# ACT instead of SP issues the eleven writes of the second group's first transform

## The chip, the cores and the metric

The kernel runs on one core of one Trainium2 chip. The metric is the time of one execution in microseconds (us). The engines are named as in the profile: PE (matrix multiplication, with PEld for its weight loads), DVE (elementwise), ACT (activation functions and copies), POOL (here index work and the transfers with indices) and SP (here only an issuer of transfers). Each engine works through its own instructions strictly in their order. A transfer (DMA) is issued by an engine and then runs on the core's 16 DMA engines; a trailing q (SPq, ACTq) marks such issues and waits in the rows.

## What is computed

The kernel first convolves each of 8 sequences of 2496 tokens with a filter in the frequency domain, and then sends every token through the one expert of 8 that a router picks for it:

```python
def _attn_ref(x, filt_r, filt_i):                  # x: 8 x 2496 x 256
    X = np.fft.rfft(x, axis=1)
    F = (filt_r + 1j * filt_i)[None, :, :]
    return np.fft.irfft(X * F, n=x.shape[1], axis=1)

def _moe_ref(x, expert_emb, tau, w1, w2):          # x: 19968 x 256
    ...
    logits = xn @ en.T / tau                       # normalized tokens and experts
    expert_idx = np.argmax(logits, axis=1)
    ...
    for e in range(E):                             # E = 8, F = 1024
        mask = expert_idx == e
        h = np.maximum(x[mask] @ w1[e], 0.0)
        out[mask] = gate_w[mask, None] * (h @ w2[e])
```

## The kernel before, in words

**Groups and transforms.** The 8 sequences are 8 groups (numbered 0 to 7), one sequence each. The Fourier transform over 2496 = 64 x 39 points is made of two small dense transforms in each direction, so that a group passes through three stages, which hand data to each other through scratch tensors in device memory:

- `conv_s1(g)`, the first transform, 11 steps: a tile of x is loaded (tiles `in`, L395), multiplied on PE (L435), copied out of PSUM by ACT into a tile `st` (L461, printed as `s`), and written to the scratch tensor SD (L463). This L463 is what the change touches.
- `conv_s2(g)`, 10 steps: a tile `a` is read back from SD (L475), multiplied (L435), filtered on DVE with a filter tile `f` (L482), transformed back (L551) and written to ZD (L555).
- `conv_sb(g)`: reads ZD, makes the token rows `y`, routes them, and POOL scatters the rows into a table XS ordered by expert (L787).

**Experts.** Tokens are then taken from XS in blocks ("slots"). A slot's rows are read transposed by SP (tile `xT`, for the first eight slots `xTf`, L867) with a small tile `meta` (`metaf`, L868) of row numbers and gate weights. PE multiplies them with the first weight matrix (`ph`, L955), ACT and DVE make the two halves of `h` (L961, L962), PE multiplies with the second matrix (`po`, L975), ACT scales (L982), and POOL scatters the result to the output (L983).

**The head.** While group 0 and the first transform of group 1 are worked off, no expert work is there yet; this stretch is `head()`. In it SP also loads the expert weights, 1 MB at a time (L257, tile W, 14 of them; the last expert's come as 8 pieces `wraw`, L264), and PE (L279, L289: `gram`), DVE (L284, L285, L293 to L300, L324) and ACT (L317) split each matrix into a high and a low 16-bit half. The expert work may use a matrix only after that. After the head, slots and the stages of the later groups alternate in `run_slots()`, group g+1's transforms beside group g's slots.

**What sets the order.** Each engine's order of instructions is decided when the kernel is built, by a scheduler that places instructions by estimated times; in the head the order on ACT, PE, DVE and SP follows the code. Each engine then waits on semaphores. Two rules matter here. The tiles rotate: `cin` has 4 buffers, so the load of tile t+3 in `conv_s1` waits until PE has used tile t-1; `st` has 3 buffers, shared with the tile `dg` of the weight preparation. And the transfers that SP and ACT issue share eight completion semaphores in turn, so that an issue also waits until the transfer that had its semaphore last has landed.

The four lines of `conv_s1` on which it turns:

```python
            st = cst.tile([P, 2, D], F32, tag="st", name=f"s{g}_{t}")
            nc.scalar.copy(st, pt)
            for h, k, m in whole(g, buf_at(g, SD[g]), t, freqs, 120):
                nc.sync.dma_start(m, st[:k, h])
```

Of the kernel before, what the change touches and what calls it, by code (L numbers as in the profile page):

```python
# [66 lines left out]
def full_blocks(tokens, size):  # L67

    return max(0, -((E * (size - 1) - tokens) // size))
# [3 lines left out]
def moe_spectral_kernel(  # L73
# [17 lines left out]
    nc = tc.nc  # L91
# [11 lines left out]
    for g, (n, size) in enumerate(GROUPS):  # L103
# [4 lines left out]
        k = full_blocks(least, size)  # L108
# [247 lines left out]
    def widths(g):  # L356

        return NAG * GROUPS[g][0] // 2, NK2 * GROUPS[g][0] // 2


    def whole(g, ap, t, rows, full):

        if GROUPS[g][0] == 2:
            k = rows(t)
            return [(slice(0, 2), k, ap(t, k, False))]
        if rows(2 * t) == rows(2 * t + 1):
            return [(slice(0, 2), full, ap(t, full, False))]
        return [(slice(j, j + 1), rows(2 * t + j), ap(2 * t + j, rows(2 * t + j), True)) for j in range(2)]

    def x_at(g):  # L370
        def at(t, k, half):
            if GROUPS[g][0] == 2:
                return x[first[g]:first[g] + 2, t * TOK:t * TOK + k].rearrange("b p c -> p b c")
            if half:
                return x[first[g], t * TOK:t * TOK + k].unsqueeze(1)
            return x[first[g], t * 2 * TOK:(t + 1) * 2 * TOK].rearrange("(j p) c -> p j c", j=2)
        return at

    def buf_at(g, buf):
        def at(t, k, half):  # L380
            if GROUPS[g][0] == 2:
                return buf[t * 120:t * 120 + k].rearrange("p (j c) -> p j c", j=2)
            if half:
                return buf[t * 120:t * 120 + k].unsqueeze(1)
            return buf[t * 240:(t + 1) * 240].rearrange("(j p) c -> p j c", j=2)
        return at
# [4 lines left out]
    def load(q, g, pool, tag, t, ap, rows, full):  # L391
        it = pool.tile([P, 2, D], F32, tag=tag, name=f"{tag}{g}_{t}")
        got = []
        for h, k, m in whole(g, ap, t, rows, full):
            q.dma_start(it[:k, h], m)  # L395
            got.append((h, it[:k, h].rearrange("p j c -> p (j c)")))
        return got
# [3 lines left out]
    def split(hi, lo, pieces):  # L401

        got = []
        for h, a in pieces:
            k, w = a.shape
            o = h.start * D
            xh, xl = hi[:k, o:o + w], lo[:k, o:o + w]
            nc.scalar.copy(xh, a)  # L408
            nc.vector.tensor_tensor(out=xl, in0=a, in1=xh.bitcast(F32), op=ALU.subtract)  # L409
            got.append((h, (xh, xl)))  # L410
        return got

    def pair(nm):
        return [cw.tile([P, 2 * D], F32R, tag="hl", bufs=XYB, name=f"{nm}_{i}") for i in range(2)]
# [6 lines left out]
    def parts_of(c, tag):  # L421

        k = c.shape[0]
        tmp = cw.tile([P, P], F32R, tag="hl", bufs=XYB, name=f"{tag}t")[:k]
        lo = const.tile([k, P], F32R, tag=f"{tag}l", name=f"{tag}l")
        nc.scalar.copy(tmp, c)
        nc.vector.tensor_tensor(out=lo, in0=c, in1=tmp.bitcast(F32), op=ALU.subtract)
        hi = const.tile([k, P], F32R, tag=tag, name=f"{tag}h")
        nc.scalar.copy(hi, tmp.bitcast(F32))
        return hi, lo  # L430

    def product(out_, c, a):

        if not isinstance(a, tuple):
            nc.tensor.matmul(out_, c[:a.shape[0]], a, start=True, stop=True)  # L435
            return
        (ch, cl), (xh, xl) = c, a
        k = xh.shape[0]
        for n, (w, b) in enumerate(((ch, xh), (cl, xh), (ch, xl))):
            nc.tensor.matmul(out_, w[:k], b, start=(n == 0), stop=(n == 2))  # L440

    def conv_s1(g):

        NTL, _ = widths(g)
        if g == G_S1:
            cons["c1"] = parts_of(cons["c1"], "c1")
        xin = {t: load(nc.gpsimd if g > 1 else nc.sync, g, cin, "in", t, x_at(g), tokens, TOK) for t in range(INB - 1)}
        if g == 1:
            yield 0
        for t in range(NTL):  # L450
            if t + INB - 1 < NTL:
                xin[t + INB - 1] = load(nc.gpsimd if g > 1 else nc.sync, g, cin, "in", t + INB - 1, x_at(g), tokens, TOK)
            if g >= G_S1:
                u = t
                xin[u] = split(*pair(f"xp{g}_{u}"), xin[u])
            pool, tag = (ps_h, "h") if g == 1 else (ps_c, "c")
            pt = pool.tile([P, 2, D], F32, tag=tag, name=f"s1_{g}_{t}")
            for h, xt in xin.pop(t):
                product(pt[:, h].rearrange("p j c -> p (j c)"), cons["c1"], xt)
            st = cst.tile([P, 2, D], F32, tag="st", name=f"s{g}_{t}")  # L460
            nc.scalar.copy(st, pt)  # L461
            for h, k, m in whole(g, buf_at(g, SD[g]), t, freqs, 120):
                nc.sync.dma_start(m, st[:k, h])  # L463
            yield W_S1

    def conv_s2(g):
# [533 lines left out]
    def later(g):  # L1000

        yield from conv_s2(g)
        if g + 1 < NG:
            s1 = conv_s1(g + 1)
            yield from both(conv_sb(g), s1, widths(g + 1)[0] / (2 * widths(g)[0] + 8))
            yield from s1
            yield -1
            yield from later(g + 1)
        else:
            yield from conv_sb(g)  # L1010
            yield -1
# [14 lines left out]
    def head():  # L1026
        yield from conv_s1(0)
        yield from conv_s2(0)
        back, ahead = conv_sb(0), conv_s1(1)
        for n, w in enumerate(back):  # L1030
            if n == XNEXT - 35:
                next(ahead)
            routed = state["routed"] * CHUNK * 2 >= NAG
            if routed and not queue:
                enqueue(0, "fixed")
            yield w
            if n >= SIDE:
                next(ahead, 0)
        yield from ahead
# [161 lines left out]
```

## Time and profile before

| | us |
|---|---|
| median of 3 runs | 1465.01 (1461.64 to 1469.56) |
| the profiled execution | 1456.85 |
| its span, first to last instruction | 1455.1 |
| PE busy | 1287.7 (88% of the span) |
| DVE busy | 958.9 (66%) |
| ACT busy | 760.4 (52%) |
| POOL busy | 512.7 (35%) |

The span starts at the first instruction of the program, and all places below are us from that start. The profiled execution is 0.56% shorter than the median; 1.75 us of it lie outside the span. Issuing a transfer does not count as busy time. A busy PE is one with a matmul in its pipeline, at either of its two clock levels (PEclk 1.00 is 2.4 GHz, 0.50 is 1.2 GHz). In a row of the timeline, a duration over several merged instructions (x5) runs from the start of the first to the end of the last, waits between them included; the brackets tell how long the engine had been idle before, and what ended that.

### The profile page before, as it was taken

The page shows a single profiled execution, that of the slowest core. Times are in us where ns is not written, and L with a number is a line of the kernel's source. Part 1 is how long each engine was busy: PE and PEld are TensorE (multiplying, and loading weights), DVE is VectorE, ACT ScalarE, POOL GpSimd, SP SyncE. Part 2 cuts the span into 40 slices and gives each one's busy share as a digit, 9 for nine tenths or more (in the row PEclk, how much of TensorE's full clock was granted, in tenths as well). Part 3 has the DMA queues.
Part 4 walks back from the last instruction along what each step waited for, and adds up shares of the span by engine and source line. Part 5 has one row for each costly group of instructions (what it writes and reads, how often), then busy time and mean ns, then how long its engine had stood idle before and what let it go on. Part 6 is the DMA issues. An engine that isn't in the chain of part 4 may idle for free. (4 is left out here: it accounts for less than half of the span.)

```text
span 1455.1 us, 36608 instructions
## 1 busy us (share of the span) xinstructions
PE 1287.7 (88%) x11006; PEld 999.8 (69%) x11006; DVE 958.9 (66%) x3126; ACT 760.4 (52%) x1756; POOL 512.7 (35%) x575
## 2 busy tenths in 40 slices
PE   6766799789877997999899988999899987999998
PEld 2243566556655775777688767877787776888997
DVE  2365796465757684978679776877686764444664
ACT  2264477345735683668456764676376622233333
POOL 0024022444344433542454245424532344112222
PEclk9877999889988997999999999999999989999999
DMA  7898879568747784779467966776575323211121
GB/s 234 285 343 295 214 223 212 149 189 235 179 122 210 211 180 118 208 187 201 120 178 208 190 145 167 220 194 157 156 195 163 93 73 73 60 45 52 42 45 41
DMA packets 275838, 240.64 MB, mean 165 GB/s; under 512 B 167946, under 2 KB 218001, under 8 KB 273857
## 3 DMA queue, kind: packets, MB, share of 16 engines
q1 hardware_dynamic: 249144, 180.33, 48.2%
q0 software_dynamic: 25360, 57.51, 12.7%
q8 instruction: 104, 1.70, 0.5%
q14 instruction: 85, 0.70, 0.2%
q10 hardware_dynamic: 1145, 0.40, 0.1%
HBM read 121.68 MB, written 85.90 MB: 143 GB/s over the span
## 5 line engine op out<-in xcount | busy, mean ns | idle before, releaser
L975 PE MATMUL po<-W,h 128*128 (+1 forms) x3864 | 517.0, 278 | 24.9 <-issue 20.4
L955 PE MATMUL ph<-xT,wp 128*128 128x256 f16 (+1 forms) x4224 | 494.5, 264 | 33.7 <-issue 23.1
L955 PEld LDWEIGHTS <-wp 128*128 128x128 f16 x4224 | 369.4, 100 | 122.9 <-issue 68.2
L975 PEld LDWEIGHTS <-h 128*128 128x128 f16 x3864 | 370.8, 99 | 106.7 <-issue 59.0
L961 ACT ACTIVATE h<-ph 128x512 f16<-128x512 f32 (+1 forms) x384 | 204.6, 533 | 334.5 <-PE ph L955 172.6
L939 DVE COPY wp<-W 128x1024 f16 x352 | 167.5, 476 | 186.9 <-PE ph L955 117.2
L983 POOL DMA_INDIRECT out_dram<-o,meta x153 | 163.2, 1067 | 351.6 <-ACT o L982 294.2
L962 DVE SCALAR_TENSOR_TENSOR h<-ph,h 128x512 f16<-128x512 f32 (+1 forms) x384 | 230.3, 600 | 58.4 <-ACT h L961 50.9
L787 POOL DMA_INDIRECT XS<-rows,ixi x176 | 181.1, 1029 | 175.1 <-issue 131.6
L395 POOL DMA_DIRECT2D in<-in_x x72 | 56.7, 789 | 161.8 <-DVE xp L409 48.1
L532 POOL TENSOR_TENSOR yy<-yy,xs 128x512 f32<-128x512 f32 x60 | 80.5, 1345 | 86.3 <-DVE xs L495 57.5
L493 DVE TENSOR_TENSOR yy<-s,f 128x256 f32<-128x256 f32 x160 | 61.2, 417 | 57.6 <-ACT xs L525 23.1
L629 DVE SCALAR_TENSOR_TENSOR rows<-y,rr,rows 128x256 f16<-128x256 f32 x176 | 77.0, 477 | 24.3 <-ACT rows L626 23.0
L982 ACT ACTIVATE o<-po,meta 128x256 f32<-128x256 f32 x153 | 66.0, 480 | 41.4 <-PE po L975 24.8
L662 ACT ACTIVATE rows<-y 128x256 f16<-128x256 f32 x176 | 67.7, 401 | 37.7 <-PE y L435 26.1
L626 ACT ACTIVATE rows<-y,rr 128x256 f16<-128x256 f32 x176 | 76.1, 495 | 15.8 <-DVE rr L667 14.8
L461 ACT COPY s<-s 128x512 f32<-128x512 f32 x88 | 52.7, 600 | 42.9 <-issue 11.5
L554 ACT COPY z<-sa 128x512 f32<-128x512 f32 x80 | 46.8, 585 | 51.5 <-PE sa L551 44.6
L440 PE MATMUL s<-xp,c1h 117*128 117x512 f32 (+1 forms) x144 | 62.5, 440 | 4.8 <-issue 3.0
L590 ACT COPY yT<-tp 128x512 f16<-128x512 f16 x99 | 58.9, 608 | 11.1 <-PE tp L588 6.4
L408 ACT CAST yp<-yy 128x512 fp32r<-128x512 f32 x50 | 30.8, 619 | 52.1 <-POOL yy L532 49.2
L495 DVE SCALAR_TENSOR_TENSOR xs<-xs,sgn_sb,f 128x256 f32<-128x256 f32 x120 | 56.6, 510 | 0.0
(198 smaller groups left out, 1657.8 us busy)
## 6 DMA issues: line engine op xcount, KB each, us to landing
f<-in_filt SPq DMA_DIRECT2D x160, 256.0 KB
a<-SD SPq DMA_DIRECT2D x80, 256.0 KB
ZD<-z SPq DMA_DIRECT2D x80, 256.0 KB
SD<-s SPq DMA_DIRECT2D x80, 240.0 KB
f<-ZD SPq DMA_DIRECT2D x80, 240.0 KB
W<-in_w SPq DMA_DIRECT2D x14, 1024.0 KB
in<-in_x POOLq DMA_DIRECT2D x60, 234.0 KB
in<-in_x SPq DMA_DIRECT2D x20, 234.0 KB
```

The costliest lines, as they stand in the source:

```text
L532: nc.gpsimd.tensor_tensor(out=yy, in0=yy, in1=xs, op=ALU.add)
L626: nc.scalar.activation(rows[:, i, 0:D], y[:, i], AF.Copy, scale=rr[:, u:u + 1])
L629: nc.vector.scalar_tensor_tensor(out=rows[:, i, D:2 * D], in0=y[:, i], scalar=rr[:, u:u + 1], in1=rows[:, i, 0:D], op0=ALU.mult, op1=ALU.s ...
L662: nc.scalar.activation(rows[:, i, D:2 * D], y[:, i], AF.Square, accum_out=ssq[:, u + i:u + i + 1])
L787: i = nc.gpsimd.indirect_dma_start(out=XS, out_offset=bass.IndirectOffsetOnAxis(ap=ix, axis=0), in_=src, in_offset=None)
L939: last["dve"] = nc.vector.tensor_copy(wp, src)
L955: last["pe"] = nc.tensor.matmul(ph[:, fi, :size], wp[:, k * 2 + wh, fi * P:(fi + 1) * P], xT[:, xh * 2 + k], start=(c == 0), stop=(c == 5))
L961: last["act"] = nc.scalar.activation(h[:, 0, :, :size], ph[:, :, :size], AF.Relu)
L962: last["lo"] = nc.vector.scalar_tensor_tensor(out=h[:, 1, :, :size], in0=ph[:, :, :size], scalar=0.0, in1=h[:, 0, :, :size], op0=ALU.max, ...
L975: nc.tensor.matmul(self.po[:, s], self.hs[fp][:, hh, fi, s * P:(s + 1) * P], self.Wp[:, off + wh * 1024:off + wh * 1024 + D], start=(fp == ...
L982: nc.scalar.activation(o, self.po[:, s], AF.Copy, scale=self.meta[:, s, 1:2])
L983: i = nc.gpsimd.indirect_dma_start(out=out, out_offset=bass.IndirectOffsetOnAxis(ap=self.meta[:, s, 0:1].bitcast(I32), axis=0), in_=o, in_ ...
```

## The change

In group 1 alone, the write of the first transform's result to SD is issued by ACT, the engine that has just made the tile, and no longer by SP. There are eleven steps; the last one's write is in two pieces, so twelve issues move.

```diff
             nc.scalar.copy(st, pt)
             for h, k, m in whole(g, buf_at(g, SD[g]), t, freqs, 120):
-                nc.sync.dma_start(m, st[:k, h])
+                (nc.scalar if g == 1 else nc.sync).dma_start(m, st[:k, h])
             yield W_S1
```

On SP, at the start of group 1's first transform (`W<-in_w` are weight loads, `in_3` to `in_5` the x tiles of steps 3 to 5, `s_0` to `s_2` the results of steps 0 to 2), the difference reads:

```order
 L257 DMA W<-in_w 128x2048 x4
 L395 DMA in_3_1208<-in_x 117x2x256
-L463 DMA SD_207<-s_0_1212 120x2x256
 L257 DMA W<-in_w 128x2048
 L395 DMA in_4_1255<-in_x 117x2x256
-L463 DMA SD_207<-s_1_1259 120x2x256
 L395 DMA in_5_1277<-in_x 117x2x256
-L463 DMA SD_207<-s_2_1281 120x2x256
 L257 DMA W<-in_w 128x2048
```

The weight load behind `in_3` no longer stands behind the write of step 0, and so on down to the first rows' read `xTf`, which stood behind the last five writes and now stands behind the load of `in_10`.

On ACT, at the same place (`ex_4` belongs to the routing of group 0), the difference reads:

```order
 L461 COPY s_0_1212<-s_1_0_1210 128x512
+L463 DMA SD_207<-s_0_1212 120x2x256
 L744 ACTIVATE ex_4_1142<-l_4_1082 128x64
 L461 COPY s_1_1259<-s_1_1_1257 128x512
+L463 DMA SD_207<-s_1_1259 120x2x256
 L590 COPY yT_9_0_1190<-tp_9_0_1185 128x512
```

Each write follows the copy that made its tile. On ACT a write also waits for the landing of the transfer that last had its semaphore, and what stands behind it on ACT waits with it: the write of step 5 waits for the landing of `in_6`, that of step 6 for the third weight load after `in_3`.

With these moves the scheduler also places other instructions differently. On DVE, at the end of the head (`metaf_1472` and `metaf_1475` are the row numbers of the first two slots, `gram_1120` and `wsc` belong to the weight preparation):

```order
 L285 TENSOR_REDUCE wmax<-dg_1414 128x2
-L324 SCALAR_TENSOR_TENSOR W<-W,wsc 128x1024 x2
+L324 SCALAR_TENSOR_TENSOR W<-W,wsc 128x1024
+L943 TENSOR_TENSOR metaf_1472<-metaf_1472,isc 128x1
+L943 TENSOR_TENSOR metaf_1475<-metaf_1475,isc 128x1
+L324 SCALAR_TENSOR_TENSOR W<-W,wsc 128x1024
 L293 TENSOR_SCALAR wall<-gram_1120 128x2
```

The gate of the first two slots, which needs their rows' `metaf`, now stands ahead of a step of the weight preparation; before, it stood some twenty instructions further down. PE changes in the same sense: the first twelve multiplications of slot 0 (`ph_0_0`) now stand right behind `s_1_10`, ahead of the `gram` sum (L289), where before they stood behind it and 49 `gram` multiplications. The orders differ once more about the second transform of group 3 and the third transform behind it, and are then the same to the end.

## Rows read from the trace of the kernel before

**Rows 1.** SP, waits from 100 to 119 us: total, times, longest.

```profile
SPq L463 <- ACT ex L744: 14.7, 1, 14.7
```

**Rows 2.** SP, timeline of the head: start, us, what it issues.

```profile
100.56 0.34 SPq L395 DMA_DIRECT2D in<-in_x  x1
117.93 0.36 SPq L463 DMA_DIRECT2D SD<-s  x1
118.33 0.43 SPq L257 DMA_DIRECT2D W<-in_w  x1
118.86 0.36 SPq L395 DMA_DIRECT2D in<-in_x  x1
...
137.63 8.94 SPq L463 DMA_DIRECT2D SD<-s  x5
146.67 1.31 SPq L867 DMA_TRANSPOSE xTf<-XS  x1
...
162.78 1.79 SPq L475 DMA_DIRECT2D a<-SD  x4
```

**Rows 3.** Stretches: busy us (x) of PE, PEld, DVE, ACT, POOL; PEclk, DMA share, GB/s.

```profile
112.00:116.00 4.00, 3.77 (x56) 3.10 (x56) 3.64 (x17) 3.13 (x10) 0.00 (x0) 1.00 0.59 207
116.00:120.00 4.00, 4.00 (x42) 2.23 (x39) 3.42 (x21) 2.43 (x6) 0.00 (x0) 1.00 0.32 72
...
132.00:136.00 4.00, 3.62 (x5) 1.27 (x5) 0.85 (x2) 1.54 (x3) 3.01 (x4) 0.50 1.03 397
...
148.00:152.00 4.00, 3.50 (x56) 3.15 (x55) 3.79 (x11) 4.00 (x5) 0.00 (x0) 1.00 0.36 72
```

**Rows 4.** PE, timeline of the head; in brackets the idle time before.

```profile
125.09 3.65 PE L435 MATMUL s<-in,c_sb 117*128 117x512 f32 x4 [3.55 <-DMA in<-in_x]
...
132.38 3.75 PE L435 MATMUL s<-in,c_sb 117*128 117x512 f32 x4 [3.48 <-DMA in<-in_x]
...
138.97 4.62 PE L435 MATMUL s<-in,c_sb 117*128 117x512 f32 x8 [2.84 <-DMA in<-in_x]
144.85 0.16 PE L289 MATMUL gram<-wmax,one 128*128 128x2 bf16 x1 [1.25 <-DVE wmax L285]
...
149.57 1.51 PE L955 MATMUL ph<-xTf,W 128*128 128x128 f16 x24
...
166.09 2.08 PE L435 MATMUL s<-a,c_sb 128*128 128x512 f32 x2 [2.76 <-DMA a<-SD]
```

**Rows 5.** POOL, timeline: first and last of the 14 scatters of this stretch.

```profile
122.01 0.99 POOL L787 DMA_INDIRECT XS<-rows,ixi  x1 [10.73 <-issue]
...
139.87 0.90 POOL L787 DMA_INDIRECT XS<-rows,ixi  x1 [0.30 <-DMA XS<-rows,ixi]
```

**Rows 6.** The same stretches' sums for three stages; columns as in rows 3.

```profile
118.00:146.00 28.00, 16.67 (x67) 7.21 (x66) 16.04 (x60) 12.31 (x21) 14.92 (x15) 0.76 0.91 316
146.00:170.00 24.00, 16.33 (x180) 13.56 (x178) 19.55 (x44) 13.34 (x17) 0.00 (x0) 0.86 0.82 214
170.00:250.00 80.00, 76.78 (x667) 51.92 (x666) 63.72 (x206) 54.18 (x134) 17.28 (x28) 1.00 0.88 220
```

**Rows 7.** ACT, timeline: an issue at the start, then copies and weight steps.

```profile
4.42 0.34 ACTq L148 DMA_DIRECT2D lt<-in_lt  x1
...
117.32 0.59 ACT L461 COPY s<-s 128x512 f32<-128x512 f32 x1 [0.93 <-PE s L435]
...
129.26 0.25 ACT L744 ACTIVATE ex<-l 128x48 f32<-128x48 f32 x1
131.36 0.20 ACT L769 CAST ixi<-ix 128x6 int32<-128x6 f32 x1 [1.85 <-issue]
...
145.73 6.35 ACT L317 ACTIVATE W<-W,wsc 128x1024 f16<-128x1024 f32 x6
```

**Rows 8.** DVE, timeline about the first slot.

```profile
148.12 0.15 DVE L293 TENSOR_SCALAR wall<-gram 128x2 f32<-128x2 f32 x1
...
152.47 0.16 DVE L943 TENSOR_TENSOR metaf<-metaf,isc 128x1 f32<-128x1 f32 x1 [0.54 <-DMA metaf<-XS]
```

**Rows 9.** PE, timeline in group 3's second transform: its two longest waits there.

```profile
443.44 0.80 PE L440 MATMUL sa<-yp,m1h 128*128 128x512 f32 x1 [5.64 <-DVE yy L493]
...
449.72 3.82 PE L955 MATMUL ph<-xT,wp 128*128 128x256 f16 x20 [2.92 <-DMA xT<-XS]
```

## The prediction, made before the changed kernel had run

> **What bounds the kernel now.** I read the page first: PE is busy for 1287.7 us of a span of 1455.1, so most of the program is bound by PE's work, and what can be won lies where PE waits. Next I read the busy times by stretches. The first 170 us are the loose part: PE is busy for 16.67 of the 28 us from 118 to 146 and for 16.33 of the 24 us from 146 to 170, and after that for 76.78 of the next 80 [rows 6]. The second group's first transform, whose writes the change moves, runs from 116 to 146 us. So the question is how much earlier the dense work at 170 us can start.
>
> Then I read SP's waits and its timeline in that stretch. SP issues `in_3` at 100.56 us, and its next issue is the write of step 0 at 117.93 [rows 2]; 14.7 us of that gap are one wait for ACT [rows 1]. ACT had only then made the tile: its copy runs from 117.32 to 117.91 [rows 7]. A weight load of 1 MB and the load of `in_4` stand behind that write and go out at 118.33 and 118.86 [rows 2]. Meanwhile the DMA engines run empty: 0.59 of their time and 207 GB/s from 112 to 116 us, 0.32 and 72 GB/s from 116 to 120 [rows 3]. After 120 us they are full, with 1.03 and 397 GB/s in the stretch at 132 [rows 3], and PE waits three times for an x tile, 3.55, 3.48 and 2.84 us [rows 4]. The first transform ends at 143.6 us (138.97 + 4.62).
>
> The same queue delays the first slots. SP's last five writes take it from 137.63 to 146.57 us, most of it waiting for ACT's copies, and the first read of rows `xTf` goes out at 146.67 [rows 2]. From there to the first read of `a` at 162.78 SP works through a chain without a hole of more than about 1 us, and PE starts the second transform at 166.09, after 2.76 us of waiting for `a` [rows 2, 4].
>
> **The change part by part.** All terms are shifts of this head.
>
> 1. SP loses twelve issues. At 0.34 to 0.36 us each [rows 2] that is 12 x 0.35 = 4.2 us of issue time, but issue time alone is not on the path, since SP waits for most of the stretch. What counts is what no longer waits behind them.
>
> 2. The weight load ahead of `in_4` goes out at about 103 us (100.56 + 0.34 + the 2.4 us or so until its semaphore is free: 117.93 less the wait of 14.7) and not at 118.33. Its 1.05 MB move while the DMA engines are less than full, and leave the full stretch. At 390 GB/s that is 2.7 us. The later weight and x loads go out up to 2 us earlier too, since they wait no longer for copies. Bounds: 2.7 us if the stretch is bound by bytes throughout; if it is bound by how late `in_6` and `in_8` stand in the queue, up to the sum of PE's three waits, 9.9 us [rows 4]. I take 4 us, near the lower end, because the DMA share is full: the first transform ends at about 139.5 us.
>
> 3. The row reads `xTf` wait no longer for the last writes, but they still wait for POOL's scatters, which the change doesn't touch. POOL issues 14 of them back to back from 122.01 to 140.77 us [rows 5]. For landing I take the 2.9 us from the issue of `xTf` (146.67) to its first use (149.57) [rows 2, 4], as the nearest row of a small transfer through XS. The first read waits for the last scatter but one, which POOL ends 1.3 us before its last, at 139.5; so the read goes out at about 142.4 and not at 146.67: 4.2 us earlier. Bounds: nothing, if the scatters land only at 146.6 (SP did not wait for them when it came there); 5.9 us, if landing takes 1.2 us.
>
> 4. SP's chain behind that, from `xTf` to the first `a`, is the same twenty issues and takes the same 16.1 us (162.78 - 146.67). So `a` goes out at 158.6 and PE starts the second transform at about 162 instead of 166.09. From 148 to 152 us the DMA engines move only 72 GB/s [rows 3], so there is room for it.
>
> 5. ACT pays twelve issues. I price them by its own at the program's start, 0.34 us [rows 7]: 12 x 0.34 = 4.1 us, and at most 0.1 us each until the copy is through. ACT is idle for 15.7 of the 28 us (28 - 12.31) [rows 6], so this is hidden except for the last two issues, which stand ahead of the dense run of weight steps from 145.73 on [rows 7]: 0.7 us, and those steps come earlier by term 2. Behind the write of step 5, which now waits on ACT for the landing of `in_6`, stand the exponential and the index cast that POOL's last six scatters need. The cast was done at 131.56 [rows 7], and POOL comes to those scatters at about 132.4 (122.01 + 8 x 1.3). If `in_6` lands by 130, this costs nothing; each us later is one us of term 3.
>
> 6. The new order on DVE and PE: DVE's gate of the first slots stood at 152.47 us and `gram`'s powers at 148.12, ahead of it [rows 8]; now the powers stand behind the gate. With rows 4.2 us earlier the gate runs at about 148.3, so the powers are about level with before. I take nothing, and keep what it costs if the rows are late (the rival below).
>
> 7. The different order in group 3: PE's two long waits there, 5.64 and 2.92 us [rows 9], are for DVE and for a row read; the read of the next slot's rows moves ahead of one `a` load, and some `a` loads move behind `meta` reads. Either sign is possible; I take zero and 3 us either way.
>
> **The sum.** The second transform and the slots start 4 us earlier (the lesser of terms 2 and 3, carried by term 4), and the dense part behind is work that PE has to do anyway, so 4 us should reach the end: 1456.85 - 4 = 1452.9 for an execution like the profiled one. The median of the runs is 8.2 us above that execution, so I put the forecast at 1465.0 - 4 = **1461 us**. That is 0.27%, less than the 0.5% that a measurement of this kernel can tell from no change.
>
> **What the skill says against it.** The stretch from 120 to 136 us already runs the DMA engines at 1.0 and more of their time [rows 3], and the change removes no byte. The Trainium skill, DMA: Bandwidth & Descriptors, section Issuing engines are not separate DMA queues, says that transfers from different engines run on the same 16 DMA engines and that issuing from several saves only the time to initiate. By that rule, a second issuer gains nothing in the full stretch. The trace agrees that the stretch is full; what it adds is that SP stood still for 14.7 us before it, with the DMA engines a third busy [rows 1, 3]. If only what happens inside the full stretch counted, the sum would be zero and the time 1465.
>
> **The rivals.** *Gain lost on the way* (1465): the full DMA stretch keeps its length, or PE and DVE, both dense from 150 to 250 us, take up the lead. For it: DVE is busy 19.55 of 24 us from 146 to 170 [rows 6], so at most 4.5 us can be won there at all. Against it: the rows and `a` come from SP's queue, and PE and DVE wait for these.
>
> *More than the shift* (1455): if in_6 and in_8 leave the queue early enough, PE's three waits mostly go, the first transform ends 7 us or so earlier, the weight preparation on ACT and DVE follows, and PE falls less often to the lower clock (PEclk 0.50 from 132 to 136 [rows 3]). Of PE's 19 idle us from 118 to 170 (11.3 + 7.7 [rows 6]) half would go: 10 us. Against it: the rows wait for POOL, which bounds the slots at term 3's 4 to 6 us.
>
> *Slower* (1470): the scatters land so late that the rows come when they came before. Then PE holds at slot 0's first multiplications until 149.57 [rows 4] with the `gram` sum behind it, which ran at 144.85, and DVE holds at the gate until 152.47, with the powers behind it, which ran at 148.12 [rows 4, 8]: the weight preparation of the next experts comes 4.4 to 5.5 us later, on engines that are dense from then on: 1465 + 5 = 1470. It decides from a read of `xTf` at about 146 us on; with a read at 144 the two effects cancel. Against it: POOL is done at 140.77, six us before. With the order of group 3 turning out badly by 3 us as well it would be 1473.
>
> **How the numbers follow.** The forecast of 1461 gets 0.45 (its own range, with the 3 us of term 7 and the spread of a median, is 1456 to 1466); gain lost 0.21; more than the shift 0.22; slower 0.12. The range must leave out no more than 2 in 10, so it takes in the lost gain whole and most of the 1455 case: 1453 to 1468. Faster by over 0.5% means under 1457.7: nearly all of the 1455 case and a fifth of the forecast's own, 0.21 + 0.09 = 0.30. Slower by over 0.5% means over 1472.3: the worse part of the slower case and a little for group 3's order, 0.10. The rest, 0.60, is no change that can be told.
>
> **What would show it.** SP's wait of 14.7 us before the write is gone and a weight load stands at 103 us; DMA's share from 104 to 116 is higher; `in_4` goes out at 117.3; the last x step ends at 139 to 140; `xTf` is issued at 142 to 143; the first `a` at 158 to 159 and the second transform starts at 162; everything after 250 us lies 4 us earlier. ACT shows twelve issues of 0.34 us and no wait of more than 2 us in them. I am wrong if `xTf` is issued at 146 or later, if a write on ACT holds it for several us and the scatters start late, or if the lead at 170 us is gone by 250 or by 650.

## The result, and the profile after

| | before | after |
|---|---|---|
| median, 22 runs of each on one chip | 1462.99 us (1457.29 to 1474.61) | 1473.09 us (1461.28 to 1483.13) |
| ratio to before | | 1.0058, 95% interval 1.0043 to 1.0073 |
| the profiled execution, and its span | 1456.85, 1455.1 | 1469.83, 1467.9 |
| PE, DVE busy | 1287.7, 958.9 | 1296.7, 949.1 |

The change makes the kernel slower by 0.6%, some 8.5 us. The forecast was 4 us faster, 1461 us, and the range ended at 1468: it was wrong, on the wrong side.

What the change was to do on SP, it did. SP's timeline after (start, us, what it issues) answers to [rows 2]:

```profile
103.81 0.33 SPq L257 DMA_DIRECT2D W<-in_w  x1
117.05 1.71 SPq L395 DMA_DIRECT2D in<-in_x  x2
...
142.81 1.42 SPq L867 DMA_TRANSPOSE xTf<-XS  x1
...
157.91 2.95 SPq L475 DMA_DIRECT2D a<-SD  x4
```

The weight load goes out 14.5 us earlier, `in_4` 1.8 us, the first rows 3.9 us and the first `a` 4.9 us earlier. In the two stretches that answer to [rows 3] (columns as there) the DMA engines are now nearly full from 112 us on, 0.97 and 0.87 of their time where it was 0.59 and 0.32:

```profile
112.00:116.00 4.00, 3.77 (x59) 3.21 (x60) 3.29 (x15) 3.22 (x10) 0.00 (x0) 1.00 0.97 362
116.00:120.00 4.00, 3.76 (x33) 1.79 (x31) 3.47 (x19) 2.37 (x6) 0.00 (x0) 1.00 0.87 268
...
170.00:250.00 80.00, 72.83 (x606) 49.22 (x606) 62.78 (x194) 51.22 (x125) 16.15 (x26) 0.98 0.78 209
```

The last of these rows shows the other side: from 170 to 250 us PE is busy for 72.83 us where it was 76.78 [rows 6]. PE's timeline (in brackets the idle time before) tells where:

```profile
137.62 4.71 PE L435 MATMUL s<-in,c_sb 117*128 117x512 f32 x8
...
162.01 1.12 PE L435 MATMUL s<-a,c_sb 128*128 128x512 f32 x2 [2.00 <-DMA a<-SD]
...
167.38 0.83 PE L955 MATMUL ph<-xTf,W 128*128 128x128 f16 x12 [1.49 <-DVE h L962]
...
171.70 1.10 PE L551 MATMUL sa<-yy,m_sb 128*128 128x512 f32 x2 [1.66 <-DVE xs L495]
...
223.25 2.07 PE L435 MATMUL y<-f,csb_sb 120*128 120x512 f32 x2 [4.38 <-DMA f<-ZD]
```

The second transform starts at 162.01 and not at 166.09 [rows 4], but five microseconds later PE waits for DVE, twice, and at 223 us it waits 4.38 us for the second transform's results. (Before, this last wait was 1.74 us.)

The last of the three waits is not DVE's. These are SP's rows before, where the second transform's last result is written to ZD and read back:

```profile
215.32 0.32 SPq L555 DMA_DIRECT2D ZD<-z  x1
218.57 1.81 SPq L395 DMA_DIRECT2D f<-ZD  x4
```

and after:

```profile
214.01 0.32 SPq L555 DMA_DIRECT2D ZD<-z  x1
219.27 1.81 SPq L395 DMA_DIRECT2D f<-ZD  x4
```

The write still goes out 1.3 us earlier than before, and the first read behind it 0.7 us later. So a part of the lead is lost in DVE's stretch, up to 214 us, and another part in this wait for the transfer. DVE is late in its stretch for a reason that stands in its own timeline:

```profile
149.82 0.15 DVE L293 TENSOR_SCALAR wall<-gram 128x2 f32<-128x2 f32 x1
...
161.25 0.16 DVE L943 TENSOR_TENSOR metaf<-metaf,isc 128x1 f32<-128x1 f32 x1 [3.52 <-DMA metaf<-XS]
...
162.07 2.48 DVE L324 SCALAR_TENSOR_TENSOR W<-W,wsc 128x1024 f16<-128x1024 f32 x2
```

The kernel before has the same weight step and the same gate in the opposite order; its rows at this place, which did not stand ahead of the prediction, are:

```profile
156.72 2.47 DVE L324 SCALAR_TENSOR_TENSOR W<-W,wsc 128x1024 f16<-128x1024 f32 x2
...
165.32 0.16 DVE L943 TENSOR_TENSOR metaf<-metaf,isc 128x1 f32<-128x1 f32 x1 [1.74 <-DMA metaf<-XS]
```

DVE used to do five weight steps (L324) from 156.72 us on and came to the second pair of gates (L943, the rows of the next two slots) at 163.6 us, when those rows were almost there. Now it comes to that pair at 157.7 us, waits 3.52 us, and starts on these steps at 162.07, 5.35 us later. The powers behind the *first* pair of gates, at which I had looked, are only 1.7 us later (149.82 against 148.12 [rows 8]). In the scheduler's order the second pair has moved as follows (- before, + after):

```
 L294 TENSOR_SCALAR wq<-wall 128x2
+L943 TENSOR_TENSOR metaf_1599<-metaf_1599,isc 128x1
 L297 TENSOR_SCALAR wsc<-wq 128x1 x2
+L943 TENSOR_TENSOR metaf_1602<-metaf_1602,isc 128x1
 L299 RECIPROCAL winv<-wsc 128x2
 L300 TENSOR_TENSOR isc<-winv 128x1
 L324 SCALAR_TENSOR_TENSOR W<-W,wsc 128x1024 x2
...
-L943 TENSOR_TENSOR metaf_1599<-metaf_1599,isc 128x1
-L943 TENSOR_TENSOR metaf_1602<-metaf_1602,isc 128x1
```

On ACT the writes themselves are as cheap as priced, 0.32 to 0.37 us each and 0.60 for the last; what I had not priced are the waits of the copies. ACT's timeline answers to [rows 7]:

```profile
117.67 0.37 ACTq L463 DMA_DIRECT2D SD<-s  x1
...
123.69 0.58 ACT L461 COPY s<-s 128x512 f32<-128x512 f32 x1 [2.69 <-DMA SD<-s]
...
128.88 0.58 ACT L461 COPY s<-s 128x512 f32<-128x512 f32 x1 [4.61 <-DMA SD<-s]
...
131.08 0.24 ACT L744 ACTIVATE ex<-l 128x48 f32<-128x48 f32 x1 [0.40 <-issue]
133.16 0.20 ACT L769 CAST ixi<-ix 128x6 int32<-128x6 f32 x1 [1.84 <-DVE rows L761]
```

The copies of steps 3 and 4 wait for the write that last used their buffer of `st` to land, and the exponential stands 1.8 us later than before (131.08 against 129.26). Later in the program, PE's two long waits of group 3 are there again, 5.16 and 3.06 us against 5.64 and 2.92 [rows 9]:

```profile
447.57 0.80 PE L440 MATMUL sa<-yp,m1h 128*128 128x512 f32 x1 [5.16 <-ACT yp L408]
...
454.53 4.45 PE L955 MATMUL ph<-xT,wp 128*128 128x256 f16 x24 [3.06 <-DMA xT<-XS]
```

To see where the time goes I compared the start of the same scaling on ACT (L982) in both traces: 166.26 against 170.11 us (3.8 early), 269.09 against 266.62 (2.5 late), 474.91 against 472.06 (2.9 late), 528.02 against 517.17 (10.9 late), 1030.56 against 1020.92 (9.6 late). The lead is lost between 170 and 270 us, and most of the lag comes between 472 and 517 us, in group 3. Two profiled executions are one draw each, so this only names the places to test. How far draws differ shows in the first copy of the second group's first transform (L461): it stands at 117.32 us before and 117.05 after, but between 112.96 and 119.78 us in all the profiles of this study.

### The profile page after: what moved, and what is told of

Its sections match the earlier page's. It is cut to its first block, busy times and chain, and to the rows that moved or that the text cites. A ratio compares the mean times of both kernels' runs of the same rounds, so it can differ in the third digit from the quotient of the medians.

```text
span 1467.9 us, 36596 instructions
## 1 busy us (share of the span) xinstructions
PE 1296.7 (88%) x11006; PEld 1003.3 (68%) x11006; DVE 949.1 (65%) x3126; ACT 761.4 (52%) x1756; POOL 509.5 (35%) x575
## 4 chain that ended last, share of the span: by engine, by line
PE 59%; issue 13%; DMA 10%; DVE 6%; ACT 5%; another core or an unknown queue 3%; POOL 2%; SPq 1%; POOLq 0%; ACTq 0%; DVEq 0%
PE ph L955 21%; PE po L975 20%; PE s L440 4%; DMA f<-ZD 3%; PE sa L551 2%; PE s L435 2%; PE y L435 2%; DMA yT<-rows 2%; PE y L440 2%; PE sa L440 2%; POOL out_dram L983 2%; DMA in<-in_x 1%; PE tp L588 1%; PE lp L604 1%
## 5 line engine op out<-in xcount | busy, mean ns | idle before, releaser
L975 PE MATMUL po<-W,h 128*128 (+1 forms) x3864 | 519.2, 279 | 30.2 <-issue 25.4
L975 PEld LDWEIGHTS <-h 128*128 128x128 f16 x3864 | 372.9, 100 | 115.9 <-issue 67.4
L939 DVE COPY wp<-W 128x1024 f16 x352 | 164.3, 467 | 182.2 <-PE ph L955 110.0
L982 ACT ACTIVATE o<-po,meta 128x256 f32<-128x256 f32 x153 | 65.8, 478 | 46.5 <-PE po L975 25.4
L461 ACT COPY s<-s 128x512 f32<-128x512 f32 x88 | 52.4, 597 | 29.3 <-DMA SD<-s 11.0
L409 DVE TENSOR_TENSOR xp<-in,xp 117x512 fp32r<-117x512 f32 (+1 forms) x72 | 46.9, 656 | 22.2 <-ACT xp L408 13.5
```

The costliest lines, as they stand in the source:

```text
L939: last["dve"] = nc.vector.tensor_copy(wp, src)
L975: nc.tensor.matmul(self.po[:, s], self.hs[fp][:, hh, fi, s * P:(s + 1) * P], self.Wp[:, off + wh * 1024:off + wh * 1024 + D], start=(fp == ...
```

## The experiments

The change has three parts: who issues the writes, the scheduler's other order up to some 240 us (the early order), and its other order from 420 to 650 us (the late order). To take them apart, the order of instructions on each engine was written into the kernel, from a table of instruction numbers, with edges that fix an order and add no wait:

```diff
-    run_slots()
+    run_slots(); pin_order(nc, tc, ORDER)
...
+        for a, b in zip(names, names[1:]):
+            tc.add_manual_dep(known[b], a, mybir.DependencyInfo(mybir.DependencyClass.NoSync,
+                                                                mybir.DependencyReason.DATA), reason="order")
```

Every ratio below is to the kernel before on the same chip at the same time, with its 95% interval. The kernels were measured in four sets, each on one chip.

### Who issues, and which order: eight combinations

**Writes on ACT, old order everywhere** (the change's line, and the table of the kernel before). 

> ACT issues the twelve writes as in the change, but on every engine all other instructions are held to the order that they had before. Theory A (the later times come from the scheduler's new order, mostly in group 3 from 420 to 650 us): the head's 4 us are there and nothing is lost behind, so 1459 to 1463 against 1463 of before, ratio 0.997 to 1.000. Theory B (the issue on ACT itself costs: its waits for landings hold copies, weight steps and the routing): slower by about as much as the change, 1469 to 1473, ratio 1.004 to 1.007.

Measured: 0.9981 (0.9954 to 1.0007).

**Writes on ACT, early order of the change, old late order** (the same, with the table for the part from 420 us on). 

> The change with its own order up to about 240 us, and the order of before in the stretch that differed from 420 us on. Theory A: 1460 to 1465, ratio 0.998 to 1.001, so most of the 8.5 us are gone. Theory B: 1469 to 1473. Theory C (the new order at the end of the head, with the gates ahead of the weight steps, costs): also 1469 to 1473, but then the kernel with ACT's writes and the old order everywhere is fast.

Measured: 1.0013 (0.9991 to 1.0036).

**Writes on SP, the change's order everywhere** (line L463 as before, the table of the change). 

> SP issues the writes as before, and every other instruction is held to the changed kernel's order. Theory A: slower than before by the cost of the order alone, without the head's gain: 1470 to 1477, ratio 1.005 to 1.010. Theory B: as before, 1461 to 1465. Theory C: 1468 to 1474.

Measured: 1.0031 (1.0013 to 1.005).

**Writes on SP, only the late order of the change.** 

> SP issues the writes as before, the order up to 240 us is that of before, and from 420 us on it is that of the changed kernel. Theory A: 1468 to 1473, ratio 1.004 to 1.007, with the loss between 440 and 540 us. Theories B and C: 1461 to 1465, as before.

Measured: 1.0013 (0.9993 to 1.0032).

**The change itself, again** (no edit). 

> The change once more, with the order of instructions that the scheduler gives it, so that it stands beside the other kernels on one chip. The runs so far give ratios to before of 0.998 for the writes on ACT in the old order, 1.001 with the new order up to 240 us as well, and 1.003 for the new order alone with the writes on SP. If the parts add up (theory A, the order from 420 us on, 0.13%, and theory C, the order up to 240 us, 0.2%, with the issue on ACT at -0.2%), the change stands at 1.001 to 1.003. If its first measurement of 1.0058 holds on this chip too, 1.004 to 1.007, then the writes on ACT and the new order cost more together than apart (theory D, an interaction).

Measured: 1.0037 (1.0002 to 1.0073), with 1.0058 the first time; below I use the mean, 1.0048.

**Writes on ACT, only the late order of the change.** 

> The writes on ACT, the order of before up to 240 us, the change's order from 420 us on. Theory A (the late order costs by itself, 0.13% by the runs so far): 0.998 + 0.001, so 0.999 to 1.001, and PE's waits for DVE and the row read at 440 to 455 us longer than in the kernel before. Theory C (the early order costs): 0.998, as the writes on ACT in the old order. Theory D (the two cost together what neither costs apart): 1.003 to 1.006 if it is the late order that meets the writes on ACT badly; 0.998 to 1.000 if it is the early one.

Measured: 1.0007 (0.9968 to 1.0046).

**Writes on SP, only the early order of the change** (here POOL's rows of group 3 stand in the change's order too, and in the run just above a part of them in the old one). 

> The writes on SP as before, the change's order up to 240 us, the old order from 420 us on. Here DVE and PE hold at the first slots' gate with the powers and the sum of squares behind it, while the rows come no earlier. Theory C (the early order costs, more so when the rows are late): 1.002 to 1.004, with a profile that lies 3 to 5 us behind before at 170 us. Theory A: 0.999 to 1.001, and a lag at 170 us that is gone by 250 us.

Measured: 1.003 (0.9998 to 1.0062).

| early order, late order | writes on SP | writes on ACT |
|---|---|---|
| old, old | 1 | 0.9981 |
| new, old | 1.0030 | 1.0013 |
| old, new | 1.0013 | 1.0007 |
| new, new | 1.0031 | 1.0048 |

Each part has four pairs in this table that differ in it alone. Their mean: the early order +0.30% (0.30, 0.18, 0.32, 0.41), the late order +0.19% (0.13, 0.01, 0.26, 0.35), the issue on ACT -0.06% (-0.19, -0.17, -0.06, +0.17). Single entries are uncertain by 0.2 to 0.4%, and each mean by some 0.17%, if the errors of the entries are independent. The early order is positive in all four pairs, the late order is just clear of nothing, and the issue on ACT costs nothing that can be told. So theory C holds, theory A probably holds too, and theory B is not borne out. That the early order costs more than the late one is not shown.

### What in the early order costs

**DVE's four gates alone, everything else as before.** The edit is the order of four instructions on DVE: the second pair as in the fence above, the first pair as in the order shown with the change. 

> The kernel before, with its writes on SP and its own order, except for four instructions on DVE: the two gates (L943) of the first slots stand one weight step earlier, ahead of the first powers, and the two gates of the next slots stand ahead of the powers' last steps and four weight steps instead of behind them, as in the changed kernel. Theory C1 (the gates on DVE are what the early order costs): DVE waits 3 to 4 us at the second pair with the weight steps behind, PE then waits in the dense stretch from 167 us on, and the ratio is 1.002 to 1.004. Theory C2 (PE's order, the multiplications of the first slot ahead of the sum of squares, is what costs): 1.000 to 1.001. Theory C3 (only both together cost): 1.000 to 1.001 here too.

Measured: 1.0045 (1.0018 to 1.0071). That is above all four values of the whole early order (0.18 to 0.41%), within the uncertainty. DVE's waits from 146 to 170 us (total, times, longest) in this kernel:

```profile
DVE metaf L943 <- DMA metaf<-XS: 10.8, 4, 4.6
```

In the kernel before the total is 2.6 us, and 6.2 us in the changed kernel.

**PE's part alone: the first slot's multiplications ahead of the sum of squares.**

```
 L435 MATMUL s_1_10_1417<-in_10_1379,c_sb 128x256 x2
+L955 MATMUL ph_0_0_1547<-xTf_1471,W 128x128      (twelve, from behind L279 gram_1564)
 L289 MATMUL gram_1120<-wmax,one_142 128x2
```

> The kernel before, with the twelve multiplications of the first slot (L955, ph_0_0) put on PE directly behind the first transform, ahead of the sum of squares, as in the changed kernel; nothing else moves. The rows come at about 149.5 us as before, so the sum of squares that ran at 144.85 waits for them behind the multiplications. Theory C2: 1.002 to 1.004, DVE's powers 4 to 5 us later than 148.1. Theory C1: 1.000 to 1.001, with a wait on PE at 149 us that is made up by 170.

Measured: 1.0001 (0.9978 to 1.0023). PE's order costs nothing by itself that can be told. ACT's part of the early order (it makes the first half of `h` after three weight steps, at 149.27 us, where it made six of them first) and SP's part, behind 165 us, were not tested alone.

**The first pair of gates alone**, then **the second pair alone**, both with the writes on SP. 

> The kernel before with only the two gates of the first slots moved on DVE, one weight step and the powers ahead of where they stand. This is the place that my rival named: the rows come at 151 to 152 us here, so the powers that ran at 148.1 run at 153 to 154. If this pair is what costs in the kernel with all four gates moved (1.0045): 1.002 to 1.004. If the second pair costs: 1.000 to 1.001, the 5 us being made up in the holes up to 170. On SP some reads of the last slots' rows also stand a place earlier, after 1300 us; I take that as nothing.

Measured: 1.0004 (0.9971 to 1.0037).

> The kernel before with only the two gates of the next slots moved on DVE, ahead of the powers' last steps and of four weight steps. Their rows come at 165.3 us, so the weight steps that ran from 156.7 to 163 run after 165.5, some 8 us later, in front of a stretch where PE and DVE are dense. If this pair is what costs: 1.002 to 1.005, with PE waiting for weights or for DVE's x tiles between 166 and 180 us. If the first pair costs: 1.000 to 1.002. The reads of the last slots' rows on SP as in the kernel with the first pair.

Measured: 1.0073 (1.0047 to 1.0098), more than expected and the highest ratio of the study. (In both kernels one row read for the last slots also stands elsewhere on SP, after 1300 us; as both have it, it does not touch the difference between them.) The DVE timeline of the second one shows the mechanism:

```profile
158.53 0.15 DVE L294 TENSOR_SCALAR wq<-wall 128x2 int32<-128x2 int32 x1
166.79 0.16 DVE L943 TENSOR_TENSOR metaf<-metaf,isc 128x1 f32<-128x1 f32 x1 [8.11 <-DMA metaf<-XS]
...
167.53 2.48 DVE L324 SCALAR_TENSOR_TENSOR W<-W,wsc 128x1024 f16<-128x1024 f32 x2
```

and PE's what follows from it:

```profile
169.61 0.40 PE L975 MATMUL po<-W,h 128*128 128x256 f16 x1 [5.19 <-ACT h L961]
171.66 1.44 PE L955 MATMUL ph<-xTf,W 128*128 128x128 f16 x12 [1.66 <-DVE h L962]
```

DVE stands still for 8.11 us in front of weight steps that it could have done; when the rows come, the weight steps, the halves of `h` and the second transform's filter all want DVE at once, and PE waits. The first scaling on ACT stands at 177.03 us, 6.9 us later than before, and at 176.52 in the kernel with all four gates moved. With the first pair alone the powers came at 154.36 us, 6.2 us late, and it cost nothing that can be told: DVE worked on without a hole behind them and reached the second pair at 169.10 without a wait, and the scaling on ACT that stands at 170.11 us in the kernel before was level.

**The change with the four gates put back**, all else as the scheduler has it. 

> The changed kernel as the scheduler orders it, except for the same four instructions on DVE, which go back to where the kernel before has them. Theory C1: the weight steps at 157 to 165 us are on time again, the lead of 4 us at the second transform lives on to 250 us, and of the loss of 0.4 to 0.6% some 0.3% come back: 1.000 to 1.003. Theory C2: 1.003 to 1.006, as the change.

Measured: 1.0039 (1.0013 to 1.0064); I had expected at most 1.003. Against the change's 1.0048 that is no gain that can be told. In the profile the gates' wait is gone, DVE does the weight steps at 157.71 and 160.18, and PE's two waits for DVE behind 165 us are gone with it. The scalings on ACT lead by 4.0 us at 170, 3.8 at 421 and 4.8 us at 472 (467.24 against 472.06). But this profile led by 4.4 us already at the transform's first copy (112.96 against 117.32), so it shows only that with the gates put back nothing is lost between 170 and 472 us. At 517 the lead is gone (517.36 against 517.17): what is left of the cost stands in group 3.

**The same with the late order of before as well.** 

> The writes on ACT, the change's order up to 240 us except for DVE's four gates, which stand where the kernel before has them, and the order of before from 420 us on. In the kernel with the gates put back alone, the profile kept its lead of 4 to 5 us from 170 to 472 us and lost it between 472 and 517, where the late order stands; its ratio was 1.0039. If gates and late order together are the loss: the lead of 4 us lives to the end, 0.996 to 0.999. If something else of the changed kernel costs (the issue on ACT with PE's early order): 1.001 to 1.004.

Measured: 1.0005 (0.9977 to 1.0033): with both undone the loss is gone, without the gain that I expected if these two were all of it. From the changed kernel's 1.0048, then, the gates alone give back 0.09%, the late order alone 0.35% (the entry of 1.0013 in the table), and both together 0.43%, each uncertain by some 0.3%. Which of the two weighs more in the changed kernel itself stays open. Between 472 and 517 us the six profiles with the late order of the change (the changed kernel's own among them) lose 4.2 to 8.7 us against the trace of before; the seven without it in the first three sets of runs lie between 0.4 us won and 3.5 us lost. In two of the six the loss is made up by 1020 us, so its worth at the end is less than that, the 0.2% of the table. What in the late order costs was not taken apart: from 465 to 535 us PE is busy for 68.84 us before and 66.68 after, so most of the 8 us there is other work that the order puts first, and not PE waiting.

**A wait that no experiment separates.** PE's wait for ZD at some 220 us goes with the writes on ACT. In the nine profiles of kernels with at most one write on ACT (the kernel before among them) it is 1.2 to 1.8 us; in the nine with eleven or twelve writes on ACT it is 1.6 to 5.4 us, and over 3 us in seven of them. The wait is also long with the early order of before (4.34 us where all writes are on ACT and the order is old everywhere, 3.49 us where only the late order is new), so it does not need the gates' new place. Its cause was not tested. It may be a cost of the issue on ACT, which the table's mean for that part then holds together with the gain in the head.

### Is there a faster version?

**Only step 0's write on ACT**, old order.

```diff
-                (nc.scalar if g == 1 else nc.sync).dma_start(m, st[:k, h])
+                (nc.scalar if g == 1 and t == 0 else nc.sync).dma_start(m, st[:k, h])
```

> Of the twelve writes only step 0's is issued on ACT, the others stay on SP, and the order of before is kept everywhere. SP's wait of 14.7 us is then gone, the weight load goes out at about 103 us and in_4 at 117, while ACT's later copies and the exponential don't wait for writes on ACT's own queue. If the early weight load is what is worth something (my term 2): the exponential and the index cast stay at 129 and 131 us, POOL's scatters end by 140 us, and the ratio is 0.995 to 0.999. If the full stretch keeps its length whatever goes ahead of it: 0.999 to 1.001. Theory B (any write issued on ACT costs there): 1.000 to 1.002.

Measured: 0.9997 (0.9969 to 1.0025). The weight load goes out at 107.67 us and `in_4` at 119.21, just ahead of the first write (119.83), but SP's last five writes still hold the rows: `xTf` is issued at 150.53. The early weight load alone is worth nothing that can be told.

**All writes but that of step 5 on ACT**, old order (`t != 5` in the same place). In the run with all writes on ACT in the old order, the condition of the prediction's term 5 had come true: the write of step 5 stood until 133.43 us for the landing of `in_6`, and the exponential behind it came 4.5 us late: 2.1 us by this hold and the rest because the copy ahead of it was late already. Its ACT timeline shows the hold:

```profile
133.43 0.32 ACTq L463 DMA_DIRECT2D SD<-s  x1
133.80 0.24 ACT L744 ACTIVATE ex<-l 128x48 f32<-128x48 f32 x1 [2.08 <-DMA in<-in_x]
```

POOL's last scatters then came late, and `xTf` went out at 147.26 us. 

> The writes on ACT except that of step 5, which SP issues; the order of before everywhere. In the run with all writes on ACT in the old order, the write of step 5 was held on ACT until 133.43 for the landing of in_6, and the exponential and the index cast behind it came 4.5 us late, so the first read of rows went out at 147.26 and nothing was won. If that hold is what ate the gain (term 5 of my prediction): the exponential stands at 130 to 132, the scatters end by 142, the read of rows goes out at 143 to 145, and the ratio is 0.995 to 0.998, below both kernels. If the copies' waits for their own writes on ACT cost as much: the read at 146 to 148 and 0.998 to 1.000.

Measured: 0.9968 (0.994 to 0.9995). The exponential stands at 131.03, and in SP's timeline the rows' read goes out 2.3 us earlier than before:

```profile
144.39 1.31 SPq L867 DMA_TRANSPOSE xTf<-XS  x1
```

**The same kernel again.** 

> The fastest kernel so far once more: the writes on ACT except that of step 5, the order of before. Its first ratio was 0.9968 (0.994 to 0.9995). If that is a gain and not the spread of the runs: 0.995 to 0.998 again, with the first read of rows at 143 to 145 us and the second transform at 162 to 164. If it was spread: 0.999 to 1.001.

Measured: 0.999 (0.9964 to 1.0016), with `xTf` at 143.5 us. Between gain and spread this doesn't decide; the three measurements with (nearly) all writes on ACT in the old order have a mean of 0.998, 3 us, uncertain by some 0.16%. That is near the 4 us of my sum and under the 0.5% that one measurement can tell. A version with four buffers of `st`, whose copies might wait less, was not run.

## Why the prediction was wrong

**Term 1** (SP loses twelve issues, nothing on the path): right.

**Term 2** (the weight load at 103 us, the first transform ends 4 us earlier): the issue came true, the end did not. The first transform's last multiplications end at 142.33 us (137.62 + 4.71) and not at 143.6: 1.3 us. The stretch stays full, and now the copies wait for buffers too. The prediction also read the time before it too favourably: of the 14.7 us in which SP stood still the DMA engines were full for the larger part (1.01 of their time from 104 to 108 us and 0.95 from 108 to 112), and less than full only behind that. Here the rule from the Trainium skill that the prediction weighed (DMA: Bandwidth & Descriptors, Issuing engines are not separate DMA queues) did better than my 4 us: a second issuer shortened the full stretch by little, and the run with the early weight load alone gave 0.9997.

**Terms 3 and 4** (`xTf` at 142.4, `a` at 158.6, the second transform at 162): right in the numbers, 142.81, 157.91 and 162.01, and in that the read now waits for POOL's scatters. That it came out so close is luck in part: the last scatter but one ended at 140.81 and not at 139.5, because the exponential was late, and the read went out 2.0 us behind it and not 2.9. That the sum took the lesser of terms 2 and 3 was unnecessary: PE does not wait for the end of the first transform but for rows and for `a`.

**Term 5** (issues hidden on ACT): right in the size of the issues. It left out the copies' waits for their buffers, 2.69 and 4.61 us, which put the exponential 1.8 us late. The hold of step 5's write did not happen in the changed kernel's profile and did in four others, the old order's among them (for the landing of `in_6` in two of the four, for a reason that the profile doesn't show in the other two). Counted from the transform's first copy, the rows' read went out 29.4 us later before, 25.8 to 27.1 us in the five profiles with eleven or twelve writes on ACT and no such hold of more than 0.5 us, and 27.8 to 30.0 us in these four. So the hold ate most or all of term 3.

**Term 6** (the new order on DVE and PE costs nothing) is the step that failed. I checked the first pair of gates and the powers behind it, found them level to within 2 us, and stopped. The second pair, in the same piece of the order, had moved ahead of five weight steps, and its rows are two reads further down SP's chain, so that an `xTf` 4 us earlier could not cover it: in the changed kernel the pair's rows were 4.1 us early (161.25 against 165.32), DVE came to it 5.9 us early (157.7 against 163.6), and it waited 3.52 us. Measured: 0.45 and 0.73% for the four gates or that pair alone in the kernel before, and 0.30% for the early order as a whole, 4.4 us, which is as much as the whole gain that I forecast. Putting the gates alone back in the changed kernel gave 0.09%, which can't be told from nothing, so how much of its loss is theirs stays open.

**Term 7** (the late order, zero, 3 us either way) was mis-sized, and it is the second step that failed: +0.19%, 2.8 us, the bad end of its bounds, and 0.35%, some 5 us, when it alone is undone in the changed kernel. The mechanism behind it stays open.

**The sum** by the measured terms: -3 us for the issue on ACT in the old order (the mean of three, two of them without step 5's write), +4.4 and +2.8 us for the two orders: +4.2 us. The change was measured at +7 us (0.48% of 1463). The difference is inside the uncertainty of the entries; whether the parts also cost more together than apart, as the column on ACT hints (the fourth pair is the largest each time), stays open.

**The rivals.** "Slower" named the right engine and the right kind of wait, with 1470 us, but the wrong pair: by its condition, a read of `xTf` at 146 us or later, it should not have decided at 142.81, and in the run with that pair alone (1.0004) it costs nothing that can be told even with late rows. "Gain lost on the way" is part of what happened between 170 and 250 us, where my sign of failure, a lead gone by 250, came true; DVE took up a part of the lead, as it said, and the longer wait for ZD another.

## What to carry to other kernels

When a change lets a scheduler place instructions anew, the moved instructions are changes of their own: list every wait on a transfer that now stands ahead of work which used to cover it, all of them and not only the first, and price each as the time from when its engine gets there to when its data land. In this kernel four small instructions on DVE, moved alone, cost more (0.45%) than the moved issues could win (0.2%). To find out, pin the old order under the new issue, and the new order under the old issue; the two halves of the answer are then measured and not argued.

## What the runs showed of the hardware that was not expected

- The first write issued on ACT's queue kept its buffer for 6.0 us (117.67 to 123.69 in the changed kernel; 4.6 to 7.8 us in the nine other profiles with that write on ACT); in the kernel before the same write on SP's queue had landed within 3.7 us, since the copy that needs the buffer ran at 121.62 without waiting for it (issue at 117.93). Whether the queue or the fuller DMA engines (0.87 against 0.32 of their time) make the difference wasn't separated.
- The same kernel before had medians of 1456.6, 1469.1, 1467.4 and 1349.8 us beside the four sets of experiments. In the fastest set the granted clock of the profiled executions was 0.96 and not 0.92 to 0.94, and PE's idle time before the second multiplications (L975) was 2.6 us (in the kernel with the first pair moved) where the kernel before shows 24.9 us, 20.4 of them put down to "issue". What makes that set 8% faster stays open; only ratios within a set were used.
